# Feed-forward products of a fused top-k attention and tanh-shrink kernel issued as two 64-column weight tiles

## The chip, the cores and the metric

The kernel runs on one core of one Trainium2 chip. The metric is the device time of the whole program in microseconds (us), as the median of three runs; the profile comes from one further execution. A core has four compute engines, which run side by side and meet through semaphores: TensorE (PE in the profile; its weight loads are listed apart as PEld), VectorE (DVE), ScalarE (ACT) and GpSimd (POOL). SyncE (SP) issues the DMAs. All data here is 32-bit floating point once it is inside the kernel.

## The reference

```python
# q, k, v: (8 batches, 8 heads, 576 rows, 64)
scores = scale * q @ k.T                          # (8, 8, 576, 576)
kth    = the 32nd largest score of each row
scores = where(scores >= kth, scores, -1e9)
attn   = exp(scores - max) ; attn = attn / (attn.sum(-1) + 1e-9)
x      = (attn @ v), heads side by side           # (4608 tokens, 512)
h      = x @ w_in                                 # w_in: (512, 2048)
out    = (h - tanh(h)) @ w_out                    # w_out: (2048, 512)
```

## The kernel before

**Attention.** The work goes step by step; a step (`Step`) is 128 query rows of a pair of heads (or, for the last 64 rows of a sequence, 64 rows of two pairs). There are 144 steps, and the loop at the end of `run` records the instructions of all engines for each in turn; every engine then executes its own in that order. For a step n:

- `scores` (L329) fills a PSUM tile with the scores of two heads. The contraction is 64 long, so each head's product uses half of the array's rows: a 64-row tiling. There is one such PSUM tile, so the scores of step n+1 must wait until VectorE has read those of step n (its last reader is L367) and ScalarE has copied them to SBUF (L337).
- `search` finds the 32nd largest score of each row on VectorE (L359 to L382). `threshold`, `mask`, `expo` and `divide` are small operations, the masking and the exponential on GpSimd and ScalarE.
- `turn_z` and `spread_keys` transpose the weights of attention through VectorE (L496) and DRAM. In the first batch TensorE transposes instead (L533, L571).
- `values` (L561) multiplies by v. It treats the two heads of a pair as two products of 64 weight columns each: `av[half(0)]` and `av[half(1)]` go to PSUM partitions 0 to 63 and 64 to 127, with alternate instructions. This is a 64-column tiling: 128 rows by 64 columns, two tiles. `values` runs once for two steps as a rule.

**Feed-forward.** Tokens are collected into units (`Unit`) of 256 tokens, 17 of them, and two of 128 at the start. The work of a 256-token unit is a list of items, which `deal` hands out in small groups between the parts of a step, at a rate (`rate`) that is worked out from counts of steps and items, not from times. The items are:

- `ffn_h` (L612): 16 items for a 256-token unit. Each forms 128 columns of h for 256 tokens with four accumulating products (`c` over the 512 inputs), 128 by 128 weights from `w_in` against 256 columns of `xT`. After two items ScalarE takes tanh (L624) and copies h (L625), and GpSimd subtracts (L626).
- `ffn_p` and `product` (L725): 14 items. The second multiplication is done in a two by two block scheme with seven block products in place of eight (`ORDER`), with sums of blocks formed beforehand on GpSimd (`sum_up`, L699). Each item is four accumulating products, with 128 by 128 weights taken from `g` and 256 columns of `w_out` or of a sum moving. They gather in the PSUM tiles `hx` and `hy`. ScalarE copies results out (L758 to L775).

For a 128-token unit, `ffn_h` has 128 columns moving and the second multiplication is `ffn_o` (L633).

**Order around the change.** In the loop of `run`, from step 45 on (`NEAR`), a step's TensorE work stands in this order: a first share of feed-forward items (0.4), then `values` if one is due, then the scores of the next step, then three more shares (0.2 each). Before step 45 `values` comes first, ahead of the first share.

So TensorE alternates between three tilings: 64-row (scores), 64-column (values) and whole array (feed-forward, transposes). In the program before, by its order of TensorE instructions, the tiling changes 400 times: 84 times from whole array to 64-column, 29 times back, 55 times from 64-column to 64-row, 88 times from whole array to 64-row and 144 times from 64-row to whole array.

The profile shows two matmul instructions, and two weight loads, for each product of 32-bit operands.

Of the kernel before, what the change touches and what calls it, by code (L numbers as in the profile page):

```python
# [54 lines left out]
def kernel(  # L55
# [9 lines left out]
    nc = tc.nc  # L65
# [46 lines left out]
    def h_bank(k, name):  # L112
        return h_ps.tile([P, 512], FP32, tag=f"h{k}", name=name)

    def next_h(name):
        bank[0] ^= 1
        return h_bank(bank[0], name)
# [98 lines left out]
    def half(t):  # L216
        return slice(t * D, (t + 1) * D)
# [381 lines left out]

    cur = {}  # L600

    def ffn_h(u, item):

        w = u.n
        per = 2 * P // w
        for f in range(item * per, (item + 1) * per):
            j, fo = f // FJ, (f % FJ) * P
            s = f * w % 512
            if s == 0:
                cur[u] = next_h("hps")  # L610
            for c in range(CD):
                nc.tensor.matmul(  # L612
                    cur[u][:, s : s + w],
                    w_in[j][:, c, fo : fo + P],
                    u.xT[:, c, 0:w],
                    start=(c == 0),
                    stop=(c == CD - 1),
                )
        if item % 2:
            th = thpool.tile([P, 512], FP32, tag="th", name="th")  # L620
            if item % 8 == 1:
                u.g.append(gpool.tile([P, 4, 512], FP32, tag="g", name="g"))
            g = u.g[-1][:, item % 8 // 2, :]
            nc.scalar.activation(th[:], cur[u][:], AF.Tanh)  # L624
            nc.scalar.copy(g, cur[u][:])  # L625
            nc.gpsimd.tensor_tensor(g, g, th[:], ALU.subtract)  # L626
# [57 lines left out]
    def quarters(u, k):  # L684

        x = u.g[k][:].rearrange("p m (f t n) -> p m f t n", f=2, t=2)
        return [[x[:, :, f, t, :] for f in range(2)] for t in range(2)]
# [19 lines left out]
    def product(u, i, k):  # L707

        left, right = ORDER[i]
        if i == 0 and k == 0:  # L710
            cur[u] = [next_h("hx"), None]
        if i == 1 and k == 0:
            cur[u][1] = h_bank(bank[0] ^ 1, "hy")
        (a11, a12), (a21, a22) = quarters(u, k)
        lhs = {"A11": a11, "A12": a12, "A22": a22, "S1": sums[k], "S2": a11, "S3": a21, "S4": a12}[left]
        acc = cur[u][i % 2][:, 0 : 2 * P]
        fresh = i in (0, 1, 3)
        for m in range(4):
            if right in whole:
                rhs = whole[right][k][:, m, :]  # L720
            else:
                r, c = {"B11": (0, 0), "T1": (0, 1), "B21": (1, 0), "B22": (1, 1)}[right]
                f = 2 * (4 * k + m) + r
                rhs = w_out[f // FJ][:, f % FJ, c * 2 * P : (c + 1) * 2 * P]
            nc.tensor.matmul(acc, lhs[:, m, :], rhs, start=(fresh and k == 0 and m == 0), stop=(k == 1 and m == 3), skip_group_check=True)  # L725
        return acc

    SUMS = {
# [7 lines left out]
    def ffn_p(u, item):  # L736

        i, k = item // 2, item % 2
        acc = product(u, i, k)
        lo, hi = slice(0, 2 * P), slice(2 * P, 4 * P)  # L740

# [55 lines left out]
    def ffn_full(u, item):  # L797

        ffn_h(u, item)
        combine_next()  # L800
        if item in (8, 9):
            sum_up(u, 0, ("S1", "S3")[item - 8])

    def ffn(u):

        nh = CF * u.n // (2 * P)
        full = len(u.blocks) == 2
        for item in range(nh):
            f = (item + 1) * CF // nh - 1
            yield CD * (f // FJ + 1), u, lambda item=item: (ffn_full if full else ffn_h)(u, item)  # L810
        if not full:
            for part in range(CF // 2):
                yield CD * (WJ + part // 2 + 1), None, lambda part=part: ffn_small_o(u, part)
            return
        for item in range(2 * len(ORDER)):
            yield 2 * WJ * CD, None, lambda item=item: ffn_p(u, item)
# [277 lines left out]
```

## Time and profile before

| what | value |
|---|---|
| median of 3 runs | 1500.38 us (1498.82 to 1500.51) |
| the profiled execution's own time | 1499.6 us |
| its span, first to last instruction | 1497.0 us |
| mean granted TensorE clock | 0.974 of full speed |
| feed-forward matmuls (L612, L725) in the trace | 2,432 and 1,904 |
| values matmuls (L561) in the trace | 2,000 |
| VectorE idle from 700 to 1300 us, of 600 | 29.7 us |

The page lists engines by busy time, then the span in 40 slices, then the chain of work that ended last. The busy time of TensorE is a modelled one, since its instructions overlap; what is firm is when an instruction starts. A distance between starts of consecutive matmuls is therefore used below rather than a duration. The trace's counts of feed-forward and values matmuls are twice the counts of products in the program.

### The profile page before, as it was taken

How to read it: one execution, taken by the hardware profiler on the slowest of the kernel's cores; microseconds unless marked ns; L12 is line 12 of the kernel's file. 1: busy time of each engine (PE TensorE's matmuls, PEld its weight loads, DVE VectorE, ACT ScalarE, POOL GpSimd, SP SyncE). 2: the span in 40 equal slices, each digit the busy share in tenths (PEclk: the TensorE clock that was granted, in tenths of full speed). 3: DMA queues.
4: the chain of work that ended last, by engine and by line, in shares of the span. 5: the costliest groups of instructions: out<-in, count | busy, mean ns of one | idle time of the engine just before them, and what ended most of it. 6: DMA issues, size and time to landing. Idle time of an engine off the chain costs nothing.

```text
span 1497.0 us, 26829 instructions
## 1 busy us (share of the span) xinstructions
PE 1382.9 (92%) x7892; PEld 1060.6 (71%) x7892; DVE 1293.6 (86%) x4914; ACT 1023.5 (68%) x1898; POOL 1102.4 (74%) x1573
## 2 busy tenths in 40 slices
PE   4667898899999999999999999999999999999998
PEld 2455666667776677767777777777777777778887
DVE  7999998999999999999999999999999999883000
ACT  4777777778777777777777777777777777664321
POOL 3777689968787785968696869696978796766523
PEclk9788999999999999999999999999999999999999
DMA  9964113766767576675766676667666666643311
GB/s 257 354 221 170 40 24 93 183 179 171 189 169 200 140 191 178 166 192 144 179 169 196 163 185 164 176 161 194 171 179 173 166 161 186 156 126 108 98 39 45
DMA packets 257179, 241.71 MB, mean 161 GB/s; under 512 B 193536, under 2 KB 201728, under 8 KB 249856
## 3 DMA queue, kind: packets, MB, share of 16 engines
q1 hardware_dynamic: 255248, 239.69, 60.3%
q8 instruction: 65, 1.06, 0.3%
q14 instruction: 90, 0.74, 0.2%
q10 hardware_dynamic: 1776, 0.22, 0.1%
HBM read 153.99 MB, written 85.85 MB: 160 GB/s over the span
## 4 chain that ended last, share of the span: by engine, by line
PE 55%; DVE 22%; POOL 5%; DMA 3%; ACT 2%; issue 2%; SPq 1%; DVEq 0%; ACTq 0%; POOLq 0%
PE hps L612 23%; PE hx L725 10%; PE hy L725 7%; PE av L561 7%; PE scps L329 6%; DVE m L379 4%; DVE zx L496 3%; DVE top L371 3%; DVE rest L382 3%; DVE ab L365 2%; POOL z L418 2%; POOL g L699 1%; DVE ab L360 1%; DMA kin<-in_k_dram 1%; DVE top L382 1%
## 5 line engine op out<-in xcount | busy, mean ns | idle before, releaser
L612 PE MATMUL hps<-xT,w_in 128*128 128x256 f32 (+1 forms) x2176 | 472.8, 374 | 5.8 <-ACT g L625 5.5
L612 PEld LDWEIGHTS hps<-xT,w_in 128*128 128x128 f32 x2176 | 394.6, 194 | 82.5 <-issue 24.2
L418 POOL TENSOR_TENSOR z<-sc,z 128x576 f32<-128x576 f32 x288 | 404.4, 1426 | 58.9 <-ACT z L415 58.4
L626 POOL TENSOR_TENSOR g<-g,th 128x512 f32<-128x512 f32 x144 | 183.6, 1275 | 116.9 <-ACT g L625 115.8
L464 ACT ACTIVATE z<-z,rd 128x576 f32<-128x576 f32 x252 | 181.1, 767 | 92.4 <-DVE rd L457 92.2
L438 ACT ACTIVATE z<-z,nb 128x576 f32<-128x576 f32 x288 | 221.8, 775 | 14.1 <-POOL z L418 14.0
L415 ACT ACTIVATE z<-sc,tb 128x576 f32<-128x576 f32 x288 | 208.2, 775 | 29.8 <-POOL tb L396 25.8
L337 ACT COPY sc<-scps 128x1152 f32<-128x1152 f32 x144 | 160.7, 1116 | 51.7 <-PE scps L329 51.4
L371 DVE MAX8 top<-ab 128x8 f32<-128x144 f32 x864 | 194.7, 296 | 0.0
L496 DVE STREAM_TRANSPOSE zx<-z 128x1152 f32<-128x1152 f32 x126 | 171.7, 1363 | 21.9 <-ACT z L464 18.8
L329 PE MATMUL scps<-kT,qT 64*128 64x288 f32 (+1 forms) x1120 | 158.7, 431 | 32.8 <-DVE top L367 30.0
L379 DVE MAX8 m<-rest 128x8 f32<-128x168 f32 x576 | 162.0, 323 | 0.0
L379 DVE MAX8 m<-top 128x8 f32<-128x144 f32 (+1 forms) x576 | 153.2, 308 | 0.0
L329 PEld LDWEIGHTS scps<-kT,qT 64*128 64x128 f32 (+1 forms) x1120 | 87.4, 178 | 86.7 <-ACT z L415 31.8
L624 ACT ACTIVATE th<-hps 128x512 f32<-128x512 f32 x144 | 84.5, 587 | 75.2 <-PE hps L612 72.8
L725 PE MATMUL hx<-w_out,g 128*128 128x256 f32 x544 | 131.1, 391 | 0.6 <-POOL g L626 0.4
L725 PE MATMUL hy<-more,g 128*128 128x256 f32 x544 | 125.9, 382 | 0.0
L725 PEld LDWEIGHTS hx<-w_out,g 128*128 128x128 f32 x544 | 103.4, 194 | 23.6 <-issue 4.3
L725 PEld LDWEIGHTS hy<-more,g 128*128 128x128 f32 x544 | 102.1, 190 | 19.3 <-issue 5.8
L396 POOL TENSOR_SCALAR tb<-m 128x1 f32<-128x1 f32 x288 | 83.8, 299 | 35.1 <-DVE m L379 34.5
L365 DVE TENSOR_TENSOR ab<-scps,sc 128x576 f32<-128x576 f32 x144 | 107.7, 748 | 0.0
L561 PE MATMUL av<-spare,vb 128*64 128x256 f32 (+1 forms) x1056 | 97.4, 327 | 0.0
(116 smaller groups left out, 2312.3 us busy)
## 6 DMA issues: line engine op xcount, KB each, us to landing
there<-zx SPq DMA_DIRECT2D x56, 1152.0 KB, 4.7
spare<-there SPq DMA_DIRECT2D x224, 288.0 KB, 5.3
more<-kept_T SPq DMA_DIRECT2D x34, 512.0 KB, 3.7
kin<-in_k_dram SPq DMA_DIRECT2D x116, 72.0 KB, 4.0
out_dram<-ot SPq DMA_DIRECT2D x32, 256.0 KB, 2.8
there<-zx SPq DMA_DIRECT2D x14, 576.0 KB, 6.8
spare<-there SPq DMA_DIRECT2D x56, 144.0 KB, 3.2
vb<-in_v_dram SPq DMA_DIRECT2D x48, 128.0 KB, 5.0
```

Source lines behind the costliest of these rows:

```text
L329: nc.tensor.matmul(ps[rows, t, s, 0:S2], qT[g.b, g.hp + i, g.part][half(t), qs], kT[g.b, g.hp + i][half(t), ks], start=True, stop=True,)
L371: nc.vector.max(top[:, t, o : o + 8], low[:, t, i, :])
L379: nc.vector.max(m[:, t, m8], seen[i][t])
L415: nc.scalar.activation(zv[:, t, :], scf[:, t, :], AF.Relu, bias=tb[:, t : t + 1], scale=-BIG)
L418: nc.gpsimd.tensor_tensor(zv[:, t, :], scf[:, t, :], zv[:, t, :], ALU.subtract)
L438: nc.scalar.activation(x["zv"][:, t, :], x["zv"][:, t, :], AF.Exp, bias=x["nb"][:, t : t + 1], scale=scale, accum_out=den[:, t : t + 1],)
L464: nc.scalar.activation(x, x, AF.Copy, scale=rds[n][:, g.i, t : t + 1])
L496: nc.vector.transpose(tiles(zx, g.nq)[:, :, :, g.i, :].rearrange("p c k j -> p k c j"), z[:].rearrange("p (k c j) -> p k c j", c=NG, j=G),)
L561: nc.tensor.matmul(av[half(t), 0, cols], vb[g.b, hp][:, t, c, :] if c < J else vrs[hp][:, t, :], es[:, :, (J + 1) * t + c if c < J else J] ...
L612: nc.tensor.matmul(cur[u][:, s : s + w], w_in[j][:, c, fo : fo + P], u.xT[:, c, 0:w], start=(c == 0), stop=(c == CD - 1),)
L626: nc.gpsimd.tensor_tensor(g, g, th[:], ALU.subtract)
L725: nc.tensor.matmul(acc, lhs[:, m, :], rhs, start=(fresh and k == 0 and m == 0), stop=(k == 1 and m == 3), skip_group_check=True)
```

## The change

A helper issues a product as two, each with 64 of the 128 weight columns and the same 256 moving columns, and each writing its own 64 PSUM partitions. `ffn_h` uses it for the 256-token units (`per` is 1 there), `product` always. Products of the 128-token units, scores, transposes and values stay as they are.

```diff
+    def by_columns(acc, lhs, rhs, start, stop):
+
+        for t in range(2):
+            nc.tensor.matmul(
+                acc[half(t)], lhs[:, half(t)], rhs, start=start, stop=stop, skip_group_check=True
+            )
+
     def ffn_h(u, item):
 ...
             for c in range(CD):
-                nc.tensor.matmul(
+                (nc.tensor.matmul if per > 1 else by_columns)(
                     cur[u][:, s : s + w],
                     w_in[j][:, c, fo : fo + P],
                     u.xT[:, c, 0:w],
 ...
-            nc.tensor.matmul(acc, lhs[:, m, :], rhs, start=(fresh and k == 0 and m == 0), stop=(k == 1 and m == 3), skip_group_check=True)
+            by_columns(acc, lhs[:, m, :], rhs, fresh and k == 0 and m == 0, k == 1 and m == 3)
         return acc
```

`half(t)` is the slice from 64t to 64t+63. The 2,040 products concerned (1,088 in `ffn_h`, 952 in `product`) become 4,080.

## The prediction

> **What bounds the kernel now.** I read the page first: engines, slices, chain.
>
> ```profile
> span 1497.0 us, 26829 instructions
> ...
> PE 1382.9 (92%) x7892; PEld 1060.6 (71%) x7892; DVE 1293.6 (86%) x4914; ACT 1023.5 (68%) x1898; POOL 1102.4 (74%) x1573
> ...
> PE   4667898899999999999999999999999999999998
> ...
> DVE  7999998999999999999999999999999999883000
> ...
> PE 55%; DVE 22%; POOL 5%; DMA 3%; ACT 2%; issue 2%; SPq 1%; DVEq 0%; ACTq 0%; POOLq 0%
> ```
>
> TensorE and VectorE are both nearly full, so which of them is late has to be asked stretch by stretch. The windows view does that (busy us and instructions of each engine):
>
> ```profile
> 300.00:500.00 200.00, 184.95 (x1053) 138.77 (x1052) 199.21 (x772) 148.75 (x274) 148.93 (x226) 0.98 0.70 179
> 500.00:700.00 200.00, 191.75 (x1120) 145.91 (x1120) 196.53 (x761) 151.57 (x278) 153.59 (x226) 0.97 0.69 170
> 700.00:900.00 200.00, 196.37 (x1124) 151.97 (x1123) 191.55 (x736) 147.39 (x272) 153.62 (x225) 1.00 0.69 177
> 900.00:1100.00 200.00, 199.60 (x1174) 155.16 (x1172) 192.53 (x745) 149.69 (x278) 160.79 (x234) 1.00 0.69 176
> 1400.00:1497.00 97.00, 90.34 (x437) 77.37 (x435) 0.15 (x1) 17.82 (x39) 38.13 (x33) 0.99 0.17 46
> ```
>
> From 300 to 500 VectorE leaves 0.8 us of 200 unused and TensorE 15: VectorE sets the pace. From 700 it turns round: TensorE leaves 0.4 to 3.6 us, VectorE 7 to 8. The last 100 us are TensorE alone. The chain agrees: from 783 to 1012 us it is TensorE almost without a break, in 300 to 600 only a third of it.
>
> A busy TensorE is not one at its peak. The timeline of TensorE shows what its blocks cost (start, length, line, tiling as rows*columns, count):
>
> ```profile
> 708.32 1.95 PE L561 MATMUL av<-spare,vb 128*64 128x256 f32 x16
> 710.10 0.60 PE L561 MATMUL av<-spare,vr 128*64 128x256 f32 x4
> 710.63 1.24 PE L329 MATMUL scps<-kT,qT 64*128 64x288 f32 x8
> 711.80 3.72 PE L725 MATMUL hy<-more,g 128*128 128x256 f32 x16
> 715.36 1.89 PE L725 MATMUL hx<-w_out,et 128*128 128x256 f32 x8
> 717.18 1.24 PE L329 MATMUL scps<-kT,qT 64*128 64x288 f32 x8
> 718.35 2.00 PE L725 MATMUL hx<-w_out,et 128*128 128x256 f32 x8
> 720.18 3.62 PE L725 MATMUL hy<-more,g 128*128 128x256 f32 x16
> 723.63 1.67 PE L725 MATMUL hx<-w_out,g 128*128 128x256 f32 x7
> ```
>
> Take starts only. From 720.18 to 723.63, 16 instructions with no change of tiling at either end: 0.2156 us each. From 715.36 to 717.18, 8 that end in a change: 1.82, which is 8 x 0.2156 and 0.095: leaving a tiling. From 718.35 to 720.18, 8 that begin after one: 1.83, an excess of 0.105: entering with 128 weight columns. From 708.32 to 710.10, 16 instructions of `values`, that is 8 pairs of half-width ones: 1.78, an excess of 0.055 over 8 x 0.2156. So a pair of 64-column instructions takes the pitch of one full instruction, and entering costs half.
>
> [...]
>
> **The change part by part.**
>
> *Steady products.* 2,040 products of two instructions become 4,080 of two. By the pitch above a pair costs what one did: 0. The bound above is that long runs behave unlike `values` blocks of 20 (rival D). Below nothing is excluded: the same columns stream.
>
> *Changes of tiling.* By the recorded order of both programs the changes fall from 400 to 316. Whole array to 64-column falls from 84 to 15: 71 places where feed-forward stands ahead of `values` vanish, and 2 appear after transposes. 64-column to whole array falls from 29 to 14: 15 places of `values` ahead of feed-forward. The 123 entries into feed-forward after scores stay changes, but with 64-column loads.
>
> - Feed-forward to `values`: 0.095 + 0.055 = 0.15 us each, x71 = 10.7.
> - `values` to feed-forward: 0.095 + 0.105 = 0.20 each, x15 = 3.0.
> - Scores to feed-forward: 0.105 - 0.055 = 0.05 each, x123 = 6.2. The trace has no entry from 64-row into 64-column. Bounds: 0 [...] and 0.05; I take 0.05, since the excess was the same 0.105 from scores and from `values`, and follows the width.
> - Added: two new changes, 0.15 each, -0.3; and leaving pairs for scores, at 68 borders. The 4 `values` instructions from 710.10 to 710.63 take 0.53, two pitches and 0.099, against 0.095 for leaving full ones: 0.004 x 68 = -0.3, and up to twice that by the rounding of the view. I take -0.5.
>
> TensorE's sum: 19.1 us. What of it is on the path? I went through the chain of waits and counted the places that lie inside its TensorE pieces: 45 of the 76 feed-forward to `values` borders, 70 of the 123 entries after scores, 6 of 15 `values` to feed-forward. 45 x 0.15 + 70 x 0.05 + 6 x 0.20 = 6.75 + 3.5 + 1.2 = 11.45, less 0.35 for the added ones: 11.1. As a check: TensorE's 55% of the chain times 19.1 gives 10.5. The rest lies beside VectorE, mostly before 600 us, and only lengthens TensorE's wait at L329.
>
> Does another engine take over where TensorE gets faster? From 800 to 1000 us, wholly on the chain, it gains 3.0 us (12 x 0.15 + 23 x 0.05); VectorE has over 7 unused there. GpSimd, which TensorE awaits for 5.6 us in all from 700 to 1390 (1.7 at most, for L699), is busy 77% from 700 to 900. So the cover holds.
>
> *Other queues.* Order and waits of VectorE, ScalarE, GpSimd and SP are the same in both programs, and each of their waits on TensorE falls on the same product. No DMA moves. TensorE's own waits stand ahead of the same products.
>
> *Sum.* 1499.6 - 11.1 = 1488.5 for an execution like the profiled one, which is 0.8 under the median of the runs: **1489.3 us**.
>
> **The rivals.**
>
> B. *Another engine takes the gain.* If half of the path's saving ends in waits (scores for L367, products for GpSimd's sums), 5.5 us remain: 1494.9. For: from 300 to 700 us VectorE has only 4.3 us unused, and a long wait of TensorE is followed by slow instructions (32 of feed-forward take 8.56 us from 492.06, right after its longest wait at L329, 4.7 us, and 7.10 elsewhere on the chain), so that longer waits could cost twice. Against: 700 to 1300 leaves VectorE 29.7.
>
> C. *All of it counts.* 1500.4 - 19.1 = 1481.3. Against: the stretch to 600 us is VectorE's.
>
> D. *Slower: instruction supply.* The place is long feed-forward runs, up to 128 instructions now. TensorE would consume four instructions per 0.2156 us instead of two. The page has 65 instruction packets of 16.3 KB on queue 8; the change adds 8,160 matmuls and loads to 15,784, so about 99 packets. [...] It decides from 0.19 us per packet, or, as any loss per pair would, from 4 ns per pair: feed-forward is 40% of the chain, 599 us or 2,780 pitches, and 11.1 / 2,780 = 4.0 ns. For: no block of 64-column tiles now is longer than 40 instructions. Against: `values` of the rest rows, with 64 moving columns, runs 40 matmuls and 40 loads from 365.21 to 366.52 without a gap, three times the rate asked for; and each gap over 0.1 us within feed-forward after 300 us has a named releaser in the timeline.
>
> E. *It does nothing.* [...] only the 0.05 entries count, 3.5 on the path: 1496.9, or 1498 if these fail in part. Against: `values` goes from one tile and tensor to another without a gap.
>
> **How the numbers follow.** Forecast 0.70, its own range 1485 to 1493; B 0.13; C 0.05; D 0.07; E 0.05. A measurement of this kernel can tell 0.2%, 3 us, from no change. Under 1497.4 lie the forecast, B, C and a part of E: 0.90. Within 0.2%: 0.04, of E and of a small D. Slower: 0.06, of D. The range reaches to B and towards C and leaves out D and the far part of C: 1483 to 1497.
>
> **What would show it.** The pitch of feed-forward pairs at 0.2156 us in long runs; no gap between feed-forward and `values`; 0.055 where feed-forward follows scores; more TensorE waiting at L329 from 300 to 600 us; VectorE's unused time from 700 to 1300 smaller by about 8 us. A pitch of 0.22 or more would make it wrong, as would new gaps in long runs, or a VectorE full from 700 on with the end unmoved.

## The result and the profile after

The changed kernel takes 1491.59 us (median of 4 runs, 1489.97 to 1493.78) against 1500.45 us (4 runs): a ratio of 0.9942, 95% interval 0.9924 to 0.9959. That is 8.9 us less, where 11.1 were forecast; the interval reaches from 6.2 to 11.4 us. The profiled execution took 1491.5 us.

The page of the changed kernel, the lines that answer to those shown of before:

```profile
span 1488.7 us, 34985 instructions
...
PE 1367.4 (92%) x11972; PEld 876.8 (59%) x11972; DVE 1292.0 (87%) x4914; ACT 1023.1 (69%) x1898; POOL 1104.8 (74%) x1573
...
q8 instruction: 97, 1.59, 0.5%
...
PE 49%; DVE 33%; POOL 7%; DMA 6%; ACT 3%; issue 2%; SPq 1%; DVEq 0%; ACTq 0%; POOLq 0%
```

TensorE has half as many instructions again and 15.5 us less busy time; weight loads fall from 1060.6 to 876.8 us, since a load of 64 columns is recorded with 137 ns, one of 128 with 190. The busy times of the other engines are as they were. The two lines of the chain can't be compared share by share: they add up to 90% before and to 101% here, because the chain of before has no piece ahead of 150 us, where that of the changed kernel has much VectorE work. A stretch that both cover is 300 to 600 us: there the first multiplication (`hps`) falls from 13.1% of the stretch to 6.3%, and VectorE's L379 rises from 10.2% to 13.4%. That is a first sign that part of what TensorE saved lies beside another engine now.

The timeline of TensorE, the same stretch of the program as shown of before (start, length, line, tiling, count):

```profile
705.19 1.95 PE L605 MATMUL hx<-et,g 128*64 128x256 f32 x16 [1.73 <-POOL g L706]
706.97 1.90 PE L561 MATMUL av<-spare,vb 128*64 128x256 f32 x16
708.70 0.60 PE L561 MATMUL av<-spare,vr 128*64 128x256 f32 x4
709.23 1.24 PE L329 MATMUL scps<-kT,qT 64*128 64x288 f32 x8
710.40 3.67 PE L605 MATMUL hy<-more,g 128*64 128x256 f32 x32
713.90 1.90 PE L605 MATMUL hx<-w_out,et 128*64 128x256 f32 x16
715.73 1.24 PE L329 MATMUL scps<-kT,qT 64*128 64x288 f32 x8
716.90 1.95 PE L605 MATMUL hx<-w_out,et 128*64 128x256 f32 x16
718.68 3.62 PE L605 MATMUL hy<-more,g 128*64 128x256 f32 x32
722.13 1.90 PE L605 MATMUL hx<-w_out,g 128*64 128x256 f32 x16
```

Again by starts; the pitch is the distance from the start of one full product, or of one pair of halves, to the next. From 718.68 to 722.13, 32 instructions, that is 16 pairs: 3.45 us, a pitch of 0.2156, as with full instructions. `values` at 706.97 follows feed-forward with nothing between: 8 pairs to 708.70 in 1.73, no entry, where the same block took 1.78; and the feed-forward block ahead of it, 1.78 from 705.19, has an entry of 0.055 after its wait and no leaving. After scores, at 710.40 and 716.90, entering costs 0.05, where it was 0.105.

The windows view, busy us of TensorE and of VectorE first and third:

```profile
300.00:500.00 200.00, 182.70 (x1628) 114.14 (x1626) 199.20 (x771) 148.50 (x274) 149.29 (x227) 0.97 0.70 180
500.00:700.00 200.00, 189.99 (x1716) 119.11 (x1714) 196.52 (x757) 152.07 (x280) 154.21 (x226) 0.97 0.68 170
700.00:900.00 200.00, 195.62 (x1818) 124.26 (x1816) 193.20 (x743) 148.58 (x275) 156.06 (x228) 1.00 0.70 181
900.00:1100.00 200.00, 198.56 (x1820) 126.08 (x1818) 194.16 (x746) 150.73 (x280) 159.86 (x234) 1.00 0.70 178
```

From 300 to 700 VectorE does the same in the same time and TensorE idles 4 us more. From 700 on TensorE's idle time rises by 0.8 and 1.0 us in these windows while VectorE fits in 1.7 and 1.6 us more work: there the program moves faster.

Where the time came from is seen best by following the steps. The table gives, for the copy of a step's scores (L337), when it began in the profiled execution before, and how much later or earlier it began in three others (the last two kernels, with the change in one half of the program only, are described below).

| step | before, us | changed kernel | second half only | first half only |
|---|---|---|---|---|
| 11 | 154 | -1.3 | +1.7 | +0.5 |
| 47 | 467 | -0.9 | +1.7 | +2.1 |
| 77 | 736 | -1.4 | +1.7 | -1.8 |
| 101 | 957 | -4.0 | -0.9 | -1.6 |
| 125 | 1173 | -5.8 | -2.7 | -1.6 |
| 142 | 1335 | -7.1 | -4.1 | -1.6 |
| end of span | 1497 | -8.3 | -5.2 | -1.5 |

The first product in two columns runs at 225 us, so what stands at step 11 is the spread of the start. From step 14 to 50 the changed kernel is 0.9 us ahead at almost every single step: it gains nothing there. Between step 77 and the end it gains 6.9 us.

### The profile page after: what moved, and what is told of

It is laid out like the page before. It is cut to its first block, busy times and chain, and to the rows that moved or that the text cites. A ratio compares the mean times of both kernels' runs of the same rounds, so it can differ in the third digit from the quotient of the medians.

```text
span 1488.7 us, 34985 instructions
## 1 busy us (share of the span) xinstructions
PE 1367.4 (92%) x11972; PEld 876.8 (59%) x11972; DVE 1292.0 (87%) x4914; ACT 1023.1 (69%) x1898; POOL 1104.8 (74%) x1573
## 4 chain that ended last, share of the span: by engine, by line
PE 49%; DVE 33%; POOL 7%; DMA 6%; ACT 3%; issue 2%; SPq 1%; DVEq 0%; ACTq 0%; POOLq 0%
PE hps L605 19%; PE hx L605 9%; PE hy L605 7%; DVE m L379 6%; PE scps L329 5%; PE av L561 5%; DVE top L371 4%; DVE zx L496 4%; DVE rest L382 4%; DVE ab L365 2%; POOL z L418 2%; DVE top L382 2%; DMA there<-zx 2%; DVE ab L360 2%; POOL g L706 2%
## 5 line engine op out<-in xcount | busy, mean ns | idle before, releaser
L418 POOL TENSOR_TENSOR z<-sc,z 128x576 f32<-128x576 f32 x288 | 405.4, 1430 | 61.2 <-ACT z L415 60.6
L605 PE MATMUL hps<-xT,w_in 128*64 128x256 f32 x3840 | 436.2, 383 | 5.4 <-ACT g L632 5.1
L605 PEld LDWEIGHTS hps<-xT,w_in 128*64 128x64 f32 x3840 | 271.7, 138 | 163.6 <-issue 23.7
L329 PE MATMUL scps<-kT,qT 64*128 64x288 f32 (+1 forms) x1120 | 161.0, 438 | 39.4 <-DVE top L367 33.2
L337 ACT COPY sc<-scps 128x1152 f32<-128x1152 f32 x144 | 160.8, 1117 | 46.2 <-PE scps L329 45.5
L379 DVE MAX8 m<-rest 128x8 f32<-128x168 f32 x576 | 161.1, 320 | 0.0
L379 DVE MAX8 m<-top 128x8 f32<-128x144 f32 (+1 forms) x576 | 152.2, 305 | 0.0
L329 PEld LDWEIGHTS scps<-kT,qT 64*128 64x128 f32 (+1 forms) x1120 | 88.4, 180 | 97.6 <-ACT z L415 33.9
L605 PE MATMUL hx<-w_out,g 128*64 128x256 f32 x1088 | 131.8, 392 | 1.6 <-POOL g L633 1.6
L605 PE MATMUL hy<-more,g 128*64 128x256 f32 x1088 | 125.3, 380 | 0.0
L605 PEld LDWEIGHTS hx<-w_out,g 128*64 128x64 f32 x1088 | 78.2, 141 | 49.9 <-issue 6.3
L605 PEld LDWEIGHTS hy<-more,g 128*64 128x64 f32 x1088 | 76.8, 137 | 42.9 <-issue 5.4
L422 POOL TENSOR_SCALAR bad<-top,tb 128x3 uint8<-128x3 f32 x288 | 96.6, 343 | 0.2
```

Source lines behind the costliest of these rows:

```text
L329: nc.tensor.matmul(ps[rows, t, s, 0:S2], qT[g.b, g.hp + i, g.part][half(t), qs], kT[g.b, g.hp + i][half(t), ks], start=True, stop=True,)
L337: nc.scalar.copy(sc[:], ps[:, :, :, 0:S2])
L379: nc.vector.max(m[:, t, m8], seen[i][t])
L418: nc.gpsimd.tensor_tensor(zv[:, t, :], scf[:, t, :], zv[:, t, :], ALU.subtract)
L605: nc.tensor.matmul(acc[half(t)], lhs[:, half(t)], rhs, start=start, stop=stop, skip_group_check=True)
```

## Experiments

Times are medians, with the ratio to the kernel before and its 95% interval.

### Half of the change at a time

First only `ffn_h`, with the product in `product` left as it was; then the other way round.

```diff
 # only the first multiplication: in product()
-            by_columns(acc, lhs[:, m, :], rhs, fresh and k == 0 and m == 0, k == 1 and m == 3)
+            nc.tensor.matmul(acc, lhs[:, m, :], rhs, start=(fresh and k == 0 and m == 0), stop=(k == 1 and m == 3), skip_group_check=True)
 # only the second: in ffn_h()
-                (nc.tensor.matmul if per > 1 else by_columns)(
+                nc.tensor.matmul(
```

> Only the first multiplication (the products of hps) in two of 64 columns. Theory 1 (changes of tiling and loads are what was saved): changes fall from 400 to 380 only, since the two multiplications now differ from each other; the sum on TensorE from 75.0 to 69.0 us, 2.8 in the time: 1497.7. Theory 2 (each narrow product gains by itself): 1,088 of 2,040 products, so 53% of 8.9 us: 1495.8.

> Only the second multiplication (the products of hx and hy) in two of 64 columns. Theory 1: changes fall from 400 to 386, the sum on TensorE from 75.0 to 70.3 us, 2.2 in the time: 1498.3; the two halves alone come to 5 us, less than the 8.9 of both together. Theory 2 (each narrow product gains by itself): 47% of 8.9: 1496.3, and the two halves add up to 8.9.

Measured: 1497.49 us (0.9980, 0.9973 to 0.9987) and 1501.92 us (1.0008, 0.9998 to 1.0017), against 1500.72. The first is 3.2 us faster, the second isn't told from no change, and together they bring nowhere near the 8.9 of the whole. A gain that belonged to the narrow products would have added up. With only one multiplication narrow and the other in full width, the border between the two is itself a change of tiling: in the timeline of the kernel with the first alone narrow, 8 full-width products of the second between scores and the first multiplication take 1.92 us from 946.32, that is 0.195 over eight pitches, and the 24 narrow pairs behind them 5.23, where 24 pitches are 5.17. That the second alone brought nothing is a miss: 2.2 us were expected, and its interval ends at a gain of 0.3. The count by halves of the program, below, gives 1.4; what took the rest stays open.

### Taking the shared tiling away again

`values` in tiles of 32 columns, so that its loads get shorter still but its tiling is no longer that of feed-forward.

```diff
-                for t in range(2):
+                for t, d in ((0, 0), (0, G), (1, 0), (1, G)):
                     nc.tensor.matmul(
-                        av[half(t), 0, cols],
-                        vb[g.b, hp][:, t, c, :] if c < J else vrs[hp][:, t, :],
+                        av[t * D + d : t * D + d + G, 0, cols],
+                        (vb[g.b, hp][:, t, c, :] if c < J else vrs[hp][:, t, :])[:, d : d + G],
```

> The changed kernel with each product of the values as two of 32 columns, so that feed-forward and values differ in tiling again, with narrower loads than before. Theory 1 (changes of tiling are what was saved): changes rise from 316 to 402, their sum on TensorE from 55.5 to 66.1 us; at the changed kernel's share of 0.46 some 5 us slower than the changed kernel, 1496.5. Theory 2 (two narrow products stream better than one wide, whatever stands beside them): no slower than the changed kernel, 1491.6.

Measured: 1496.83 us (0.9977, 0.9968 to 0.9986). In the timeline of this kernel feed-forward and `values` come apart again:

```profile
946.11 5.35 PE L605 MATMUL hps<-xT,w_in 128*64 128x256 f32 x48
951.39 1.93 PE L561 MATMUL av<-spare,vb 128*32 128x256 f32 x32
953.14 0.61 PE L561 MATMUL av<-spare,vr 128*32 128x256 f32 x8
```

The same blocks in the changed kernel:

```profile
944.49 5.35 PE L605 MATMUL hps<-xT,w_in 128*64 128x256 f32 x48
949.67 1.90 PE L561 MATMUL av<-spare,vb 128*64 128x256 f32 x16
951.39 0.60 PE L561 MATMUL av<-spare,vr 128*64 128x256 f32 x4
```

24 pairs take 5.28 us where they must leave the tiling, 5.18 where they need not, and `values` takes 1.75 after entering with 32 columns, 1.72 without entering. So what the kernel gained from is the tiling that stays the same across these borders, and not the narrow form: with the border put back, 5.2 of the 8.9 us are gone (some 5 were expected).

### Scores and everything else in narrower tiles

Scores with 64 query rows in a product, on the kernel before and on the changed one; and all of feed-forward and `values` in tiles of 32 columns.

```diff
 # scores
-            for i in range(2 if g.rem else 1):
+            for i in range(2):
...
-                        ps[rows, t, s, 0:S2],
-                        qT[g.b, g.hp + i, g.part][half(t), qs],
-                        kT[g.b, g.hp + i][half(t), ks],
+                        ps[half(i), t, s, 0:S2],
+                        qT[g.b, hp, g.part][half(t), q0 : q0 + D],
+                        kT[g.b, hp][half(t), ks],
 # all in 32 columns: values as above, and in by_columns()
-        for t in range(2):
+        for t in range(4):
...
-                acc[half(t)], lhs[:, half(t)], rhs, start=start, stop=stop, skip_group_check=True
+                acc[group(t)], lhs[:, group(t)], rhs, start=start, stop=stop, skip_group_check=True
```

> The kernel before with each product of the scores as two of 64 query rows. Theory 1 (the exposed first load goes with its width): 6.3 us on TensorE, 2.9 in the time: 1497.5. Theory 2 (the load isn't what delays the first pitch): the first pitch in a scores block stays 0.349 us and the time 1500.4.

> The changed kernel with each product of the scores as two of 64 query rows, so that the first weight load of each scores block is of 64 columns instead of 128. Theory 1 (the exposed first load goes with its width): each of 123 blocks starts 0.05 us sooner, 6.4 us on TensorE, 2.9 of it in the time: 1488.7; the first pitch in a scores block falls from 0.349 to about 0.299. Theory 2 (with the changed kernel the other engines set the pace and TensorE's savings no longer count): 1491.6.

> The changed kernel with feed-forward and values products in four of 32 columns each, one tiling for both. Theory 1: the same 316 changes, with a first load of 0.027 us instead of 0.055; 3.7 us less on TensorE, 1.7 in the time: 1489.9; the steady pitch stays 0.2156 us. Theory 2 (eight instructions in a pitch are more than can be supplied, or four tiles don't overlap): the pitch of feed-forward rises and the time goes over 1500.

Measured: 1498.96 us (0.9988, 0.9981 to 0.9994), 1488.65 us (0.9923, 0.9910 to 0.9936) and 1492.24 us (0.9941, 0.9927 to 0.9955). The second is the fastest kernel of this study by its median; its interval overlaps that of the changed kernel. One block of scores in the timeline of the changed kernel:

```profile
941.54 1.24 PE L329 MATMUL scps<-kT,qT 64*128 64x288 f32 x8
942.71 1.95 PE L605 MATMUL hx<-w_out,g 128*64 128x256 f32 x16
```

The same block in the timeline of this kernel:

```profile
940.08 1.20 PE L329 MATMUL scps<-kT,qT 64*64 64x288 f32 x16
941.21 1.95 PE L605 MATMUL hx<-w_out,g 128*64 128x256 f32 x16
```

The block is 0.04 shorter, 1.13 after 1.17, not 0.05. The instructions one by one tell why. A group here is the two products, or four half ones, that are issued together. The first pitch falls by 0.053, from 0.346 to 0.293, but the distance from the last group of tiles to the next block's start grows by 0.014, from 0.339 to 0.353. The timeline of the kernel in 32 columns shows the same at feed-forward:

```profile
935.06 3.66 PE L605 MATMUL hy<-more,g 128*32 128x256 f32 x64
938.53 1.91 PE L605 MATMUL hx<-w_out,g 128*32 128x256 f32 x32
940.38 1.24 PE L329 MATMUL scps<-kT,qT 64*128 64x288 f32 x8
941.55 1.93 PE L605 MATMUL hx<-w_out,g 128*32 128x256 f32 x32
943.30 5.36 PE L605 MATMUL hps<-xT,w_in 128*32 128x256 f32 x96
```

From 941.55 to 943.30, 8 groups of four in 1.75: an entry of 0.025, half of the 0.05 with 64 columns. From 938.53 to 940.38, 1.85: leaving takes 0.125, against 0.105 in the changed kernel and 0.095 before. What leaving costs more with four tiles takes back part of what entering costs less: 2.0 us remain on TensorE by the count below, and the six runs of this kernel can't tell that from nothing. And eight instructions in a pitch bring no gap: from 935.06 to 938.53, 16 groups take 3.47, the entry and 16 pitches of 0.2156.

### VectorE relieved

If VectorE is what kept the first half from gaining, relieving it should let the gain through. Both kernels leave out the last of four rounds of the search and take the threshold from the 24th largest score.

```diff
-            for t in range(2):
+            for t in range(2 if i < 3 else 0):
                 nc.vector.max(m[:, t, m8], seen[i][t])
-            if i < rounds - 1:
+            if i < 2:
...
-            nc.gpsimd.tensor_scalar(tb[:], m[:, :, TOP - 1], BIG, None, ALU.mult)
+            nc.gpsimd.tensor_scalar(tb[:], m[:, :, 23], BIG, None, ALU.mult)
...
```

> The kernel before with the last of four rounds of the search left out (two MAX8 and two replacements a step), so that rows keep their top 24 and VectorE has about 1.3 us a step less. It is the base of the next run. Theory 1 (the change's gain was held back in the first half because VectorE sets the pace there until about 740 us): without that, TensorE sets the pace all along; about 1440 us, from 1500 less the 28 us that TensorE waited for VectorE from 300 to 1390 and as much again before. Theory 2 (VectorE isn't what held it back): within 15 us of 1500.

> The changed kernel with the same round left out. Theory 1: the difference to the run with full-width products and the same round left out rises from 8.9 us to between 14 and 19.5, the whole of what the removed changes of tiling and the half loads come to on TensorE (75.0 us of changes before, 55.5 after). Theory 2 (the removed changes are worth only the 8.9 us that were measured, the pieces were priced too high): the difference stays between 7 and 11.

Measured: 1466.06 us and 1457.44 us, 8.6 apart. The time fell by 34 us, not 60. The difference stayed where the second theory had it, between 7 and 11, but not for its reason: the pieces were not priced too high, as the starts in the timeline show.

The steps show what the pair settles and what not. With full-width products, relieving VectorE brings 33.0 us by step 77 and 33.8 by step 137: hardly anything after about 740 us. So VectorE was on the path in the first half and hardly at all in the second. But in the relieved pair too the change gains after that point: 7.3 us from step 77 to step 142, and only 1.3 us from where it begins to step 77, of some 9 that TensorE saves there. In between it gains 2.0 us up to 531 us and has lost them again at 565. And VectorE was no longer full there. The windows view of the pair, with full-width products and then with the change:

```profile
300.00:500.00 200.00, 196.25 (x1137) 147.67 (x1136) 187.40 (x673) 159.26 (x293) 161.26 (x242) 0.99 0.74 191
300.00:500.00 200.00, 194.11 (x1760) 121.70 (x1758) 188.99 (x677) 161.74 (x298) 162.56 (x247) 0.98 0.75 191
```

VectorE has 11 to 13 us of 200 unused, and still so little comes through. So a full VectorE alone doesn't explain why the first half gains nothing. GpSimd stands in the chain of this pair there (L418 with 9.2% and 10.2% of it from 200 to 470 us), and TensorE waits for L367 (15.5 and 19.3 us from 200 to 740); what takes the gain isn't settled.

### The change in one half of the program

The direct test: two columns only from step 78 on, or only before it. Both take about as much off TensorE. `now[0]` is the step whose instructions are being recorded.

```diff
     def by_columns(acc, lhs, rhs, start, stop):
 
+        if now[0] < 78:   # the other kernel: now[0] >= 78
+            nc.tensor.matmul(acc, lhs, rhs, start=start, stop=stop, skip_group_check=True)
+            return
```

> Feed-forward in two of 64 columns only from step 78 of 144 on (about 740 us), full width ahead of it. Half of the removed changes and half loads remain: the sum on TensorE falls from 75.0 to 65.3 us. Theory 1 (only places where TensorE sets the pace count, and those lie after step 78): the whole gain of the changed kernel, 1491.6. Theory 2 (the places counted on the chain of waits in the first half counted too, 3.4 of 11.4 us): 70% of the gain, 1494.3. Theory 3 (any change of tiling removed counts alike): half, 1496.

> Feed-forward in two of 64 columns only up to step 78, full width from there on; the sum on TensorE falls from 75.0 to 65.6 us, as much as in the run for the second half. Theory 1: no gain, 1500.4. Theory 2: 30% of the gain, 1497.8. Theory 3: half of it, 1496.

Measured: 1494.03 us (0.9954, 0.9940 to 0.9968) for the second half, 1501.35 us (1.0003, 0.9995 to 1.0010) for the first, against 1500.28. Alone, the first half brings nothing that 21 runs can show: its interval ends at a gain of 0.8 us. That is what the first theory expected of it. For the second half the first theory expected the whole gain, 1491.6, and the second theory 1494.3; the second came true. In the profiled executions the second half gains 6.9 us from step 77 to the end, as in the changed kernel. But the halves don't add up to the whole: by the ratios they come to 6.9 and -0.5, against 8.7 for the changed kernel. With four and five runs the difference of 2.3 isn't clear of noise, so it stays open whether the first half adds something once the second is changed too.

TensorE's waits from 300 to 740 us show where the first half's saving went. The view of waits in the kernel before (total us, times, longest), in the kernel with the second half changed, which is the same in this stretch, and in the kernel with the first half changed:

```profile
PE scps L329 <- DVE top L367: 20.2, 11, 4.7
PE scps L329 <- DVE top L367: 21.7, 12, 4.7
PE scps L329 <- DVE top L367: 26.4, 13, 4.7
```

5 to 6 us more waiting for the last reader of the scores, where two executions of the same instructions differ by 1.5. In the changed kernel it is 24.2.

One observation doesn't fit. Between steps 47 and 77 the profiled execution of the kernel with the first half changed is 3.9 us quicker than that of before. Four other kernels that save on TensorE there are quicker too, by 2.3 to 2.7 us (first multiplication only, `values` in 32 columns, scores in 64 on the changed kernel, all in 32). Scores in 64 on the kernel before are 1.2 quicker, the changed kernel 0.5, the kernel with the second half changed 0.0, and the second multiplication only is 0.5 slower. Each is one execution, and the 21 timed runs of the first half don't bear a gain out. An effect of 1 or 2 us in these steps, lost again elsewhere, is therefore not ruled out.

### All runs together

Each run's changes of tiling, priced by the trace: leaving 0.093 with one tile, 0.100 with two, 0.113 with four (scores 0.096 and 0.110), entering 0.104, 0.051 and 0.024 for 128, 64 and 32 columns. "Second half" counts only what lies after step 77, about 740 us. The last column is the difference of the medians.

| kernel | sum on TensorE against before | of it second half | measured |
|---|---|---|---|
| changed | -19.0 | -9.7 | -8.9 |
| first multiplication only | -5.8 | -2.3 | -3.2 |
| second multiplication only | -4.6 | -1.4 | +1.2 |
| values in 32 columns | -7.2 | -3.7 | -3.5 |
| scores in 64, on before | -4.9 | -2.3 | -1.8 |
| scores in 64, on changed | -24.0 | -11.9 | -11.6 |
| all in 32 columns | -21.0 | -10.6 | -8.5 |
| change in the second half | -9.5 | -9.5 | -6.3 |
| change in the first half | -9.2 | +0.2 | +1.1 |

The column of the second half foretells the measured one within some 3 us throughout; the whole sum doesn't. In the first seven rows, though, the second half is close to half of the sum, so that a plain half of everything would do nearly as well there. Only the last two rows tell these two apart: half of the sum would be -4.8 and -4.6, where -6.3 and +1.1 were measured.

## Why the prediction was nearly right, and the term that was off

- **Steady products at no cost**: right. A pair keeps the pitch of 0.2156 us, in runs far longer than the 20 instructions of `values`: 256 instructions from 1429.86 us take 27.62.
- **Prices of a change**: right. Entry after scores, the one that the trace of before didn't show, is 0.05 us; of its two bounds the upper one held. The entry goes with the columns of the block's first weight load: 0.104, 0.051 and 0.024 with 128, 64 and 32. The loads with 128 and 64 columns are recorded with 190 and 137 ns, which is longer, but the difference, 53 ns, is that of their entries. In the trace of before, the first load of `values` starts together with its first product, at 708.32; in the changed kernel, where feed-forward stands ahead in the same tiling, it starts at 706.76 for the product at 706.97, beside the last pair of feed-forward. Leaving in pairs costs 0.007 more, which at 68 borders is the 0.5 that was taken.
- **Sum on TensorE**: 19.1 forecast, 19.0 by the prices measured afterwards.
- **What of it is on the path**: this is the term that was mis-sized. The result alone doesn't show it, since 11.1 lies within its interval; the run with the first half changed does. Of the 11.45 us counted on the chain, 3.55 lie ahead of 736 us and 7.9 behind it. Changing the first half alone gave nothing (+1.1, interval across zero). From step 77 to the end the profile shows 6.9. A small slip adds to it: two of the 45 borders, at 179 and 189 us, belong to units of 128 tokens, which the change leaves as they are (76 such borders were counted there, where 71 vanish); that is 0.3 us. The chain of waits was read as if all its pieces counted. In the first half it runs through TensorE for a stretch, then through VectorE, and shorter pieces of TensorE were followed by longer waits at L329 (26.4 us from 300 to 740 with the first half changed, 20.2 before). From 300 to 500 us VectorE leaves 0.8 us of 200 unused, and the prediction called it the one that sets the pace there, yet it counted the pieces of TensorE in that stretch. That VectorE's own work takes the gain is argued and not shown: with VectorE relieved, the first half gained only 1.3 us.
- **Cover by VectorE and GpSimd in the second half**: held for the most part. From 740 to 1390 us TensorE's idle time rose from 9.2 to 12.3 us; that is about the step from 9.7, the sum of the second half, to 6.9. VectorE's unused time from 700 to 1300 fell by 5.7 us, from 29.7 to 24.0; about 8 were named.
- **The rivals**: **D**, instruction supply, is out. The packets on queue 8 rose from 65 to 97, near the 99 that were worked out, with no gap in the 256 instructions above, and doubling the instructions once more in the kernel of 32 columns left the pitch at 0.2156 us. **E**, in which the borders between feed-forward and `values` cost what they did, is out: the feed-forward block at 705.19 has no leaving, and `values` behind it no entry. **B** describes what was seen in the first half, a saving that ends in waits for L367, but more than its 5.5 us remained in all. **C**, all of it, lies outside the result's interval.

The forecast is good where it was worked out from starts. That the total came within 2.2 us owes something to luck: the share on the path rests on a count along one chain, and the part of it that failed was the smaller one, 3.55 of 11.45 us.

## What to carry to other kernels

Count the changes of TensorE's tiling in the order of instructions and price them from starts in the timeline: leaving (here 0.093 to 0.113 us, with one to four tiles) and entering, which goes with the columns of the first weight load (here 0.104, 0.051 and 0.024 us with 128, 64 and 32). Products that lie between narrow ones may then be worth issuing in the narrow tiling too, all of them, since a group left in another tiling brings changes back: 402 of them with `values` in 32 columns, where the changed kernel has 316, and 5.2 us of the time. When a saving is spread evenly over the program, don't count every piece of the chain that it shortens. In a stretch where the chain passes to and fro between engines, the saving can come back as a longer wait, as it did here before 740 us (26.4 us of waits for L367 after 20.2). That another engine has idle time there isn't enough to be sure of the gain, as the relieved pair shows (11 to 13 us of 200 unused on VectorE, and a gain of 1.3 us). A run with the change in one stretch alone tells which stretches count.

## What the runs showed of the hardware that was not expected

Two or four column tiles that share the same rows and the same moving columns kept the pitch of 0.2156 us that one product in full width has, weight loads included: 4 instructions (matmuls and loads) in a pitch, then 8, where there had been 2. The tiles of a group start 6 to 7 ns after one another, and each further tile puts off leaving the tiling by about as much: from feed-forward to scores 0.309 us with one, 0.316 with two and 0.329 with four, start to start. So 32 columns instead of 64 save 0.027 us at each entry and lose 0.013 at each leaving; in the time no difference could be told (1492.24 against 1491.59 us).
